# Attention scores: one float32 product per head in place of three float32r products

## The chip, the cores and the metric

One core of one Trainium2 chip runs the whole program. The metric is the device time of one execution in microseconds (us); the kernel is launched once per execution, and of several executions the median counts. Engines are called PE (matrix products; PEld is its loading of the stationary operand), DVE (vector), ACT (scalar), POOL and SP (which issues most of the DMAs).

## What is computed

Windowed attention with global keys and a linear bias, and then two feed-forward layers with different gates:

```python
scores = scale * np.matmul(q, k.transpose(0, 1, 3, 2))   # (2, 8, 768, 64) each
scores = scores + bias                                   # -slope(head) * distance
scores = np.where(keep, scores, -1000000000.0)           # 96 local keys, 8 global ones
a = softmax(scores);  attn = np.matmul(a, v)
x = attn as (1536, 512)
x = silu(x @ w_in) @ w_out                # weights (512, 2048), (2048, 512), float64
out = (h * clip(h + 3, 0, 6) / 6) @ w2_out,  h = x @ w2_in
```

## The kernel before

The program has two stages that overlap a little. The attention (some 0 to 143 us of the profile) is cut into 16 units: a batch entry, half of the sequence (384 queries) and a pair of heads. A unit has three tiles of 128 queries, so that there are 48 steps `n` (list `seq`). After it come the feed-forward layers, whose pieces are long chains of PE products with the weights split into a high and a low float32r half; from step 16 on, every second step of the attention also carries one such piece (`h_piece`, 12 products, or `y_piece`).

A step is spread over several turns of the loop (`attention_loop`, `transposes`), and one turn issues, in this order: `stage_b` of tile n (scores into PSUM tiles `psS`, one bank per head; DVE adds the bias and takes the minimum into `z`; ACT takes exponentials); `stage_b2` of tile n-1 (DVE makes the reciprocal sums `sm`, POOL scales `z`); the deferred work in `rests`; `stage_c` of tile n-3 (four PE transposes of `z` into `psT`, copied to `pt` by DVE, or by ACT in a unit's first tile); `stage_d` of tile n-4 (products of `pt` and the values into `psO`); a feed-forward piece; and, once a unit each, `stage_a` for the keys (part 0) and the queries (part 1) of a later unit.

`stage_a` (L321) transposes three 128x128 tiles of two heads' keys or queries on PE, with the keys before the block and the 32 global keys (`kp`) as one more small transpose, into a PSUM bank `psA`. Two heads lie one above the other, in partitions 0 to 63 and 64 to 127. ACT then writes the high half (`kh` at L366 in two or three pieces, `qh` at L337 with the scale -1/8), in float32r, and one turn later DVE writes the rest to `kl` (L370, as many pieces) and `ql` (L340). Pieces: 128x384 for the own keys, 128x64 for the two copies of the global keys between them, and in second halves 128x128 for the keys before the block. `stage_b` (L379) makes three products for each of the two heads, `qh kh`, `qh kl` and `ql kh`, all of 256 key columns, alternating between the heads (L385 to L388).

Orders: PE, ACT and POOL execute in the order in which the code issues (`manual_schedule`, L799). DVE and the DMA queue of SP are ordered by the framework's scheduler while the attention runs, and by the code after it. PSUM has eight banks: two of tag `S` for the scores, three of tag `tr` that `psA` and `psT` share, two `o`, one `f`. `raw` tiles of keys, queries and weights have two buffers, and a load waits until the old content has been read.

Of the kernel before, what the change touches and what calls it, by code (L numbers as in the profile page):

```python
# [10 lines left out]
F32 = mybir.dt.float32  # L11
F32R = mybir.dt.float32r
# [3 lines left out]
ALU = mybir.AluOpType  # L16
PSUM = bass.MemoryType.PSUM

P = 128
# [9 lines left out]
def attention_ffn_kernel(ctx, tc, q, k, v, n_global, n_local, w_in1, w_out1, w_in2, w_out2, out):  # L29
    nc = tc.nc  # L30
    B, H, S, D = q.shape
# [4 lines left out]
    HB = 3  # L36
    TB = HB * P
# [19 lines left out]
    apool = first_half.enter_context(tc.tile_pool(name="att", bufs=2, side="right"))  # L57
# [4 lines left out]
    def bank(tag, name):  # L62
        return psum.tile([P, 512], F32, name=name, tag=tag, bufs=ps_bufs[tag])
# [153 lines left out]
    raw, tr = {}, {}  # L217
    G = NGLOB_MAX
    ZB = 4
    G0 = P - G  # L220
    W = 2 * P
# [77 lines left out]
    def beyond():  # L299

        fl, ng, nl = small[:, 2:5], nval[:, 0:1], nval[:, 1:2]
        nc.vector.tensor_scalar(out=fl[:, 0:1], in0=nl, scalar1=1.0, scalar2=None, op0=ALU.is_lt)
        nc.vector.tensor_scalar(out=fl[:, 1:2], in0=nl, scalar1=float(NLOC_MAX), scalar2=None, op0=ALU.is_gt)
        nc.vector.tensor_scalar(out=fl[:, 2:3], in0=ng, scalar1=float(NGLOB_MAX), scalar2=None, op0=ALU.is_gt)
        nc.vector.tensor_tensor(out=fl[:, 0:1], in0=fl[:, 0:1], in1=fl[:, 1:2], op=ALU.add)
        nc.vector.tensor_tensor(out=fl[:, 0:1], in0=fl[:, 0:1], in1=fl[:, 2:3], op=ALU.add)
        nc.vector.tensor_copy(flag, fl[:, 0:1])
# [3 lines left out]
    def biases(p):  # L311

        nbs[p] = [cpool.tile([P, 2, w], F32, name=f"{n}{p}", tag=f"{n}{p}") for n, w in (("nbB", P), ("nbA", W))]
        for nb, dist in zip(nbs[p], (distB, distA)):
            for h in range(2):
                nc.gpsimd.tensor_scalar(out=nb[:, h, :], in0=dist, scalar1=slopes[2 * p + h], scalar2=1.0, op0=ALU.mult, op1=ALU.mult)


    KW = P + HB * SP

    def stage_a(u, part):  # L321

        b, half, p = units[u]
        rk, kp, rq, rv, vp = raw[u]
        if part == 0:
            tr[u] = tuple(apool.tile([P, w], F32R, name=f"{n}{u}", tag=n) for n, w in (("kh", KW), ("kl", KW), ("qh", TB), ("ql", TB)))
        kh, kl, qh, ql = tr[u]
        ps = bank(ATAG, f"psA{u}_{part}")
        src = rq if part else rk
        for i in range(HB):  # L330
            nc.tensor.transpose(ps[:, i * P:(i + 1) * P], src[:, i].rearrange("p h d -> p (h d)"), ident)
        sub = dict(op0=ALU.mult, op1=ALU.subtract)
        if part:
            sc = -1.0 / (D ** 0.5)

            def evac():
                nc.scalar.mul(qh, ps[:, :TB], sc)  # L337

            def rest():
                nc.vector.scalar_tensor_tensor(out=ql, in0=ps[:, :TB], scalar=sc, in1=qh.bitcast(F32), **sub)  # L340

            return evac, rest
        m = TB + (P if half else G)
        kpf = kp.rearrange("p h d -> p (h d)")
        if half:
            nc.tensor.transpose(ps[:, TB:m], kpf, ident)
        else:
            nc.tensor.transpose(ps[:, TB:m], kpf[:G], ident[:G, :G])

        def tiles(x):  # L350
            return x[:, P:].rearrange("p (t c) -> p t c", t=HB)

        def own(x):
            return x.rearrange("p (t c) -> p t c", t=HB)

        def glo(x):
            return x.unsqueeze(1).to_broadcast([P, HB - 1, G])


        parts = [(lambda x: tiles(x)[:, :, :P], own(ps[:, :TB])), (lambda x: tiles(x)[:, :HB - 1, P:], glo(ps[:, m - G:m]))]  # L360
        if half:
            parts.append((lambda x: x[:, :P], ps[:, TB:m]))

        def evac():
            for at_, src in parts:
                nc.scalar.copy(at_(kh), src)  # L366

        def rest():
            for at_, src in parts:
                nc.vector.tensor_tensor(out=at_(kl), in0=src, in1=at_(kh).bitcast(F32), op=ALU.subtract)  # L370

        return evac, rest

    zt, smt, ptt, pso = {}, {}, {}, {}

    def first(u, t):
        return units[u][1] == 0 and t == 0

    def stage_b(n, u, t):  # L379
        b, half, p = units[u]  # L380
        kh, kl, qh, ql = tr[u]
        tags = ("SS", "fS", "Sf")[n % 3] if n < PRE - 1 else "SS"
        ps = [bank(tags[h], f"psS{u}_{t}_{h}") for h in range(2)]
        o = P if first(u, t) else t * SP
        for i, (a, c) in enumerate(((qh, kh), (qh, kl), (ql, kh))):  # L385
            for h in range(2):
                hs = slice(h * D, (h + 1) * D)
                nc.tensor.matmul(ps[h][:, :W], a[hs, t * P:(t + 1) * P], c[hs, o:o + W], start=i == 0, stop=i == 2)  # L388
        w, nb = (P, nbs[p][0]) if first(u, t) else (W, nbs[p][1])
        z = apool.tile([P, 2, W], F32, name=f"z{u}_{t}", tag="z", bufs=ZB)  # L390
        mn = apool.tile([P, 2], F32, name=f"mn{u}_{t}", tag="mn", bufs=3)
        sm = apool.tile([P, 2], F32, name=f"sm{u}_{t}", tag="sm", bufs=3)
        for h in range(2):
            nc.vector.tensor_tensor_reduce(  # L394
                out=z[:, h, :w], in0=ps[h][:, :w], in1=nb[:, h, :], scale=1.0, scalar=3e38,
                op0=ALU.add, op1=ALU.min, accum_out=mn[:, h:h + 1])
        for h in range(2):
            nc.scalar.activation(out=z[:, h, :w], in_=z[:, h, :w], func=AF.Exp, bias=mn[:, h:h + 1], scale=-1.0,  # L398
                                 accum_out=sm[:, h:h + 1])
        zt[u, t], smt[u, t] = z, sm  # L400

    def stage_b2(u, t):
        z, sm, w = zt[u, t], smt.pop((u, t)), P if first(u, t) else W
        nc.vector.tensor_scalar(out=sm, in0=sm, scalar1=1e-9, scalar2=None, op0=ALU.add)  # L404
        nc.vector.reciprocal(sm, sm)  # L405
        for h in range(2):
            nc.gpsimd.tensor_scalar(out=z[:, h, :w], in0=z[:, h, :w], scalar1=sm[:, h:h + 1], scalar2=1.0,  # L407
                                    op0=ALU.mult, op1=ALU.mult)
# [34 lines left out]
    queue, late, rests, now = {}, {}, {}, [0]  # L443
# [4 lines left out]
    def attention_loop(n):  # L448
        for f in queue.pop(n, []):
            f()  # L450
        if n < len(seq):
            u, t = seq[n]
            stage_b(n, u, t)
            if t == HB - 1 and u + 1 < NP:
                biases(u + 1)
        if n == 0:
            e, r = stage_a(1, 0)
            e()
            r()
            beyond()  # L460
        if 0 <= n - 1 < len(seq):
            stage_b2(*seq[n - 1])
        for f in rests.pop(n, []):
            f()
        if APOS == 0:
            transposes(n)
        if 0 <= n - CL < len(seq):
            stage_c(*seq[n - CL])
        if 0 <= n - LAG < len(seq):
            u, t = seq[n - LAG]  # L470
            f = stage_d(u, t)
            if f:
                at(n + 1, f)
                if u + 2 < len(units):
                    loads_v(u + 2)

        if APOS == 1:
            transposes(n)

    def transposes(n):  # L480
        for d, part in ((KOFF, 0), (QOFF, 1)):
            if (n + d) % HB == 0 and 1 <= (n + d) // HB < len(units):
                e, r = stage_a((n + d) // HB, part)
                e()
                rests.setdefault(n + 1, []).append(r)
                if part and (n + d) // HB + 2 < len(units):
                    loads((n + d) // HB + 2)

# [237 lines left out]
    for l, c in chunks:  # L726
        first_piece[l, c] = len(stream)
        if fast(l, c):
# [5 lines left out]
            h, y = H(l, c, 2), Y(l, c, 0)  # L734
# [3 lines left out]
        if (l, c) == (1, 0):  # L738

            h = H(l, c, 0) + H(l, c, 1) + H(l, c, 2)  # L740
# [5 lines left out]
        for tk in blocks(l, c):  # L746
            hs = [(h_piece, l, c, tk, j) for j in range(FC)]
# [14 lines left out]
    with tc.manual_schedule(engines=None):  # L762
        nc.vector.memset(three, 3.0)
        for i, ap in enumerate((n_global, n_local)):
            nc.sync.dma_start(nwords[:, i, :], ap.bitcast(I32).partition_broadcast(P))
        loads(0)
        make_identity(nc, ident)
        positions()
        loads(1)
        load_weights()  # L770
        loads_v(0)
        load_weights()
        loads(2)
        loads_v(1)
        load_weights()
        ek, rk_ = stage_a(0, 0)
        ek()
        eq, rq_ = stage_a(0, 1)
        eq()
        patterns()  # L780
        rk_()
        rq_()
        biases(0)
    todo = {when(i): f for i, f in enumerate(stream)}

# [279 lines left out]
```

## Time and profile before

| what | us |
|---|---|
| executions timed | 641.52, 641.78, 646.76 (median 641.78) |
| span of the profiled execution, first to last instruction | 638.6 |
| busy in the span: PE / PEld | 617.2 / 498.9 |
| busy in the span: DVE / ACT / POOL | 489.9 / 417.4 / 161.0 |

The profiled execution's own device time isn't listed apart from its span; the two executions that agree end some 3 us above that span. Busy times are unions of an engine's instructions; the ends of PE's products are modelled and overlap, so that a busy PE need not be at its peak: how long a group of products occupies PE is read from where it starts to where the next one starts.

### The profile page before, as it was taken

The numbers are of one execution on the slowest core, as the hardware profiler recorded it, in microseconds if no ns is written. First come the engines' busy times: TensorE is split into PE (matmuls) and PEld (weight loads), VectorE is DVE, ScalarE is ACT, GpSimd is POOL, SyncE is SP. The second block draws the span as 40 slices with busy tenths as digits, with TensorE's granted clock in tenths as the row PEclk, the third lists the DMA queues.
The fourth block names the chain that finished last, engine by engine and source line by source line (L and its number), as shares of the span: only waits on it lengthen the run. The fifth ranks groups of instructions, "written<-read, shape, count | busy, mean of one in ns | idle before, by whom it ended". The sixth has DMA issues, their size and how long they took to land.

```text
span 638.6 us, 9729 instructions
## 1 busy us (share of the span) xinstructions
PE 617.2 (97%) x3214; PEld 498.9 (78%) x3214; DVE 489.9 (77%) x1107; ACT 417.4 (65%) x887; POOL 161.0 (25%) x233
## 2 busy tenths in 40 slices
PE   5889999999999999999999998999999999999996
PEld 3667777789888788888888887887788888888885
DVE  5899889953578796767675679988979696969453
ACT  4787877765557576666666676765766666666760
POOL 2776666561111111111212120011111111111110
PEclk9999999999999999999999999999999999999999
DMA  6555645349577667777776793186576868686544
GB/s 174 136 139 136 149 112 137 99 150 204 103 162 166 144 146 176 161 180 166 181 163 134 164 198 100 66 247 150 132 173 165 182 157 181 157 176 162 100 102 166
DMA packets 81625, 97.31 MB, mean 152 GB/s; under 512 B 55456, under 2 KB 55456, under 8 KB 81312
## 3 DMA queue, kind: packets, MB, share of 16 engines
q0 software_dynamic: 12576, 45.09, 37.7%
q1 hardware_dynamic: 68992, 51.53, 26.8%
q8 instruction: 27, 0.44, 0.3%
q14 instruction: 30, 0.25, 0.1%
HBM read 46.27 MB, written 3.15 MB: 77 GB/s over the span
## 4 chain that ended last, share of the span: by engine, by line
PE 35%; issue 25%; POOL 5%; DVE 2%; DMA 2%; ACT 1%; POOLq 0%; ACTq 0%; SPq 0%; DVEq 0%
PE psY L683 19%; PE psH L510 9%; POOL y L712 5%; PE psP_b L591 3%; PE psP_c L591 2%; PE psP_a L591 2%; DMA y<-st 1%; DMA raw<-in_moe_w_in_dram 1%; ACT st L708 0%; DVE g L541 0%; DVE da L1027 0%; DVE wol L148 0%; DVE dc L134 0%; DVE u L608 0%; ACT da L103 0%
## 5 line engine op out<-in xcount | busy, mean ns | idle before, releaser
L712 POOL DMA_DIRECT2D y<-st x78 | 66.9, 857 | 362.4 <-ACT st L708 357.2
L708 ACT COPY st<-psY 128x512 f32<-128x512 f32 x156 | 91.3, 586 | 51.6 <-PE psY L683 47.5
L510 PE MATMUL psH<-xh,wih 128*128 128x512 f32 (+1 forms) x216 | 83.2, 385 | 1.7 <-DVE g L541 1.7
L510 PE MATMUL psH<-xl,wih 128*128 128x512 f32 (+1 forms) x216 | 82.5, 382 | 0.0
L510 PE MATMUL psH<-xh,wil 128*128 128x512 f32 (+1 forms) x216 | 82.4, 382 | 0.0
L683 PE MATMUL psY<-gh,woh 128*128 128x512 f32 (+1 forms) x160 | 61.4, 384 | 0.0
L683 PE MATMUL psY<-gh,wol 128*128 128x512 f32 (+1 forms) x160 | 60.6, 378 | 0.0
L683 PE MATMUL psY<-gl,woh 128*128 128x512 f32 (+1 forms) x160 | 60.5, 378 | 0.0
L398 ACT ACTIVATE z<-z,mn 128x256 f32<-128x256 f32 (+1 forms) x96 | 46.5, 486 | 21.1 <-DVE mn L394 15.6
L407 POOL TENSOR_SCALAR z<-z,sm 128x256 f32<-128x256 f32 (+1 forms) x96 | 48.2, 514 | 43.9 <-DVE sm L405 18.4
L683 PE MATMUL psY<-woh,gl 128*128 128x512 f32 x144 | 56.1, 390 | 0.1
L683 PE MATMUL psY<-woh,gh 128*128 128x512 f32 x144 | 56.1, 390 | 0.1
L683 PE MATMUL psY<-wol,gh 128*128 128x512 f32 x144 | 56.0, 389 | 0.0
L510 PEld LDWEIGHTS psH<-xh,wih 128*128 128x128 f32 x216 | 40.5, 188 | 10.6 <-DVE g L541 2.1
L103 ACT ACTIVATE da<-raw 128x512 f32<-128x512 f32 x64 | 42.9, 670 | 5.9 <-DMA raw<-in_moe_w_in_dram 5.5
L510 PEld LDWEIGHTS psH<-xl,wih 128*128 128x128 f32 x216 | 40.5, 188 | 7.5 <-DVE xl L620 0.4
L510 PEld LDWEIGHTS psH<-xh,wil 128*128 128x128 f32 x216 | 40.5, 188 | 7.1
L1027 DVE SCALAR_TENSOR_TENSOR da<-raw,da 128x512 int32<-128x512 int32 x64 | 44.3, 693 | 1.2 <-DVE sm L404 0.2
L608 DVE TENSOR_TENSOR u<-psP_c,u 128x512 f32<-128x512 f32 x22 | 15.1, 688 | 34.5 <-ACT u L602 34.5
L532 ACT ACTIVATE a<-psH 128x512 f32<-128x512 f32 (+1 forms) x24 | 14.2, 590 | 40.4 <-PE psH L510 40.3
L551 DVE SCALAR_TENSOR_TENSOR gl<-a,gh 128x512 fp32r<-128x512 f32 (+1 forms) x34 | 23.2, 682 | 21.9 <-ACT gh L545 21.6
L1015 DVE TENSOR_SCALAR da<-da 128x512 f32<-128x512 f32 x64 | 28.3, 442 | 14.7 <-ACT da L103 14.7
(185 smaller groups left out, 1565.2 us busy)
## 6 DMA issues: line engine op xcount, KB each, us to landing
y<-st POOLq DMA_DIRECT2D x78, 512.0 KB, 4.8
raw<-in_moe_w_in_dram SPq DMA_DIRECT2D x32, 512.0 KB, 4.1
raw<-in_moe_w_out_dram SPq DMA_DIRECT2D x32, 512.0 KB, 3.3
rk<-in_k_dram SPq DMA_DIRECT2D x32, 96.0 KB, 2.5
rq<-in_q_dram SPq DMA_DIRECT2D x32, 96.0 KB, 2.9
rv<-in_v_dram SPq DMA_DIRECT2D x32, 96.0 KB, 2.6
out_dram<-y SPq DMA_DIRECT2D x12, 256.0 KB, 2.0
xf<-xh SPq DMA_DIRECT2D x2, 1024.0 KB, 6.7
```

The source lines that it names most:

```text
L103: nc.scalar.activation(out=t["a"], in_=raws[n][:, :, 1].bitcast(F32), func=AF.Abs)
L398: nc.scalar.activation(out=z[:, h, :w], in_=z[:, h, :w], func=AF.Exp, bias=mn[:, h:h + 1], scale=-1.0, accum_out=sm[:, h:h + 1])
L407: nc.gpsimd.tensor_scalar(out=z[:, h, :w], in0=z[:, h, :w], scalar1=sm[:, h:h + 1], scalar2=1.0, op0=ALU.mult, op1=ALU.mult)
L510: nc.tensor.matmul(ps, a[:, kt, js], x[:, kt, n0:n1], start=n == 0, stop=n == 3 * KT - 1)
L551: nc.vector.scalar_tensor_tensor(out=gl[:, j, :], in0=t["a"], scalar=2.0, in1=gh[:, j, :].bitcast(F32), op0=ALU.mult, op1=ALU.subtract)
L591: nc.tensor.matmul(ps, a[:, 2 * k + q, f * P:(f + 1) * P], x, start=p in (1, 5) and n == 0, stop=n == 5, skip_group_check=True)
L608: nc.vector.tensor_tensor(out=u, in0=st["c"], in1=u, op=ALU.add)
L683: nc.tensor.matmul(ps[:, :rhs.shape[1]], lhs, rhs, start=n == 0, stop=n == 3 * FC - 1)
L708: nc.scalar.copy(st[:, m % 2, :], part)
L712: late.setdefault(n, []).append(lambda: nc.gpsimd.dma_start(y, st, accum_op=ALU.add))
L1015: nc.vector.tensor_scalar(out=a, in0=a, scalar1=as_float(897 << 20), scalar2=as_float((1151 << 20) - 1), op0=ALU.max, op1=ALU.min)
L1027: nc.vector.scalar_tensor_tensor(out=ai, in0=w1, scalar=-0x40000000, in1=ai, op0=ALU.bitwise_and, op1=ALU.bitwise_or)
```

## The change

Keys and queries are kept as one float32 tile each (`kt`, `qt`) instead of a high and a low float32r tile. ACT writes the own keys and the queries as before, without the cast; the narrow pieces of the keys, the global ones and those before the block, are copied by DVE in the same turn instead of by ACT; DVE's subtractions are gone. The scores of a head are one float32 product of 256 columns.

```diff
@@ stage_a @@
-            tr[u] = tuple(apool.tile([P, w], F32R, name=f"{n}{u}", tag=n) for n, w in (("kh", KW), ("kl", KW), ("qh", TB), ("ql", TB)))
-        kh, kl, qh, ql = tr[u]
+            tr[u] = tuple(apool.tile([P, w], F32, name=f"{n}{u}", tag=n) for n, w in (("kt", KW), ("qt", TB)))
+        kt, qt = tr[u]
...
-            def evac():
-                nc.scalar.mul(qh, ps[:, :TB], sc)
-
-            def rest():
-                nc.vector.scalar_tensor_tensor(out=ql, in0=ps[:, :TB], scalar=sc, in1=qh.bitcast(F32), **sub)
-
-            return evac, rest
+            nc.scalar.mul(qt, ps[:, :TB], -1.0 / (D ** 0.5))
+            return
...
-        parts = [(lambda x: tiles(x)[:, :, :P], own(ps[:, :TB])), (lambda x: tiles(x)[:, :HB - 1, P:], glo(ps[:, m - G:m]))]
+        nc.scalar.copy(tiles(kt)[:, :, :P], own(ps[:, :TB]))
+        nc.vector.tensor_copy(tiles(kt)[:, :HB - 1, P:], glo(ps[:, m - G:m]))
         if half:
-            parts.append((lambda x: x[:, :P], ps[:, TB:m]))
-
-        def evac():
-            for at_, src in parts:
-                nc.scalar.copy(at_(kh), src)
-
-        def rest():
-            for at_, src in parts:
-                nc.vector.tensor_tensor(out=at_(kl), in0=src, in1=at_(kh).bitcast(F32), op=ALU.subtract)
-
-        return evac, rest
+            nc.vector.tensor_copy(kt[:, :P], ps[:, TB:m])
@@ stage_b @@
-        for i, (a, c) in enumerate(((qh, kh), (qh, kl), (ql, kh))):
-            for h in range(2):
-                hs = slice(h * D, (h + 1) * D)
-                nc.tensor.matmul(ps[h][:, :W], a[hs, t * P:(t + 1) * P], c[hs, o:o + W], start=i == 0, stop=i == 2)
+        for h in range(2):
+            hs = slice(h * D, (h + 1) * D)
+            nc.tensor.matmul(ps[h][:, :W], qt[hs, t * P:(t + 1) * P], kt[hs, o:o + W], start=True, stop=True)
@@ transposes @@
-                e, r = stage_a((n + d) // HB, part)
-                e()
-                rests.setdefault(n + 1, []).append(r)
+                stage_a((n + d) // HB, part)
```

The calls of `stage_a` in the first turn and ahead of the loop change in the same way: before, the deferred halves `rk_()` and `rq_()` came after `patterns()`; now there are none.

## Rows read from the trace of the kernel before

**Rows 1.** The page's head: span of the profiled execution.

```profile
span 638.6 us, 9729 instructions
```

**Rows 2.** Busy time by stage (count in brackets; last: granted clock, DMA share, GB/s).

```profile
core 0: us, PE busy (x) PEld busy (x) DVE busy (x) ACT busy (x) POOL busy (x), PEclk, DMA share, GB/s
0.00:143.00 143.00, 130.02 (x1061) 96.11 (x1062) 119.84 (x453) 102.59 (x330) 90.21 (x151) 1.00 0.54 136
143.00:300.00 157.00, 156.48 (x704) 130.94 (x704) 110.61 (x198) 97.88 (x181) 24.30 (x28) 1.00 0.72 160
```

**Rows 3.** Chain that ended last, one of its feed-forward pieces: start, length, what.

```profile
422.07 2.72 PE psH L510 x12
```

**Rows 4.** Waits of PE from 20 to 143 us: total, times, longest.

```profile
PE psO L435 <- DVE pt L419: 2.9, 3, 1.1
PE psA L331 <- DMA rk<-in_k_dram: 0.9, 1, 0.9
PE psT L416 <- DVE kl L370: 0.9, 2, 0.6
PE psT L416 <- ACT pt L421: 0.5, 1, 0.5
```

**Rows 5.** Groups by line and shape, 0 to 143 us: busy us, mean ns, idle before.

```profile
L419 DVE COPY pt<-psT 128x512 f32<-128x512 f32 x32 | 21.7, 678 | 0.8 <-PE psT L416 0.8
L388 PE MATMUL psS<-kh,qh 64*128 64x256 f32 x96 | 21.2, 401 | 1.1 <-ACT qh L337 0.6 <-DVE mn L394 0.4
L435 PE MATMUL psO<-pt,rv 128*64 128x128 f32 x192 | 19.3, 277 | 0.0
...
L370 DVE TENSOR_TENSOR kl<-psA,kh 128x384 fp32r<-128x384 f32 x16 | 8.8, 548 | 0.7 <-ACT kh L366 0.7
L340 DVE SCALAR_TENSOR_TENSOR ql<-psA,qh 128x384 fp32r<-128x384 f32 x16 | 8.7, 546 | 0.0
...
L370 DVE TENSOR_TENSOR kl<-psA,kh 128x64 fp32r<-128x64 f32 x16 | 3.4, 209 | 0.0
L366 ACT CAST kh<-psA 128x64 fp32r<-128x64 f32 x16 | 3.3, 209 | 0.0
```

**Rows 6.** Timeline of PE, parts of 60 to 68 us: start, length, what.

```profile
60.70 0.64 PE L388 MATMUL psS<-kh,qh 64*128 64x256 f32 x2
...
61.51 0.66 PE L416 MATMUL psT<-ident,z 128*128 128x128 f32 x4
...
67.27 0.39 PE L388 MATMUL psS<-kh,qh 64*128 64x256 f32 x2
67.50 0.28 PE L388 MATMUL psS<-kl,qh 64*128 64x256 f32 x2
67.62 0.28 PE L388 MATMUL psS<-kh,ql 64*128 64x256 f32 x2
67.82 0.44 PE L416 MATMUL psT<-ident,z 128*128 128x128 f32 x2
```

**Rows 7.** Timeline of PE, moments at 62.10 us (first row) and 62.48 us.

```profile
62.09 0.33 PE L435 MATMUL psO<-pt,vp 128*64 128x128 f32 x2
...
62.25 0.28 PE L435 MATMUL psO<-pt,vp 128*64 128x128 f32 x2
62.36 0.39 PE L435 MATMUL psO<-pt,rv 128*64 128x128 f32 x4
```

**Rows 8.** Timeline of PE around one wait (idle time and its end in brackets).

```profile
34.91 0.66 PE L416 MATMUL psT<-ident,z 128*128 128x128 f32 x4
36.56 0.51 PE L435 MATMUL psO<-pt,vp 128*64 128x128 f32 x4 [0.99 <-DVE pt L419]
```

**Rows 9.** Timeline of DVE in that wait.

```profile
35.31 0.55 DVE L340 SCALAR_TENSOR_TENSOR ql<-psA,qh 128x384 fp32r<-128x384 f32 x1
35.77 0.15 DVE L405 RECIPROCAL sm<-sm 128x2 f32<-128x2 f32 x1
35.84 0.67 DVE L419 COPY pt<-psT 128x512 f32<-128x512 f32 x1
```

**Rows 10.** Timeline of PE, 13 to 24 us: two transposes that wait for keys.

```profile
14.97 0.87 PE L331 MATMUL psA<-ident,rk 128*128 128x128 f32 x3 [0.55 <-DMA rk<-in_k_dram]
...
23.24 0.52 PE L331 MATMUL psA<-ident,rk 128*128 128x128 f32 x3 [0.87 <-DMA rk<-in_k_dram]
```

More of the change, by code (lines that the diff above doesn't have):

```diff
@@ L331, in stage_a @@
             nc.tensor.transpose(ps[:, i * P:(i + 1) * P], src[:, i].rearrange("p h d -> p (h d)"), ident)
-        sub = dict(op0=ALU.mult, op1=ALU.subtract)
         if part:
-            sc = -1.0 / (D ** 0.5)
-            def evac():
-                nc.scalar.mul(qh, ps[:, :TB], sc)
-            def rest():
-                nc.vector.scalar_tensor_tensor(out=ql, in0=ps[:, :TB], scalar=sc, in1=qh.bitcast(F32), **sub)
-            return evac, rest
+            nc.scalar.mul(qt, ps[:, :TB], -1.0 / (D ** 0.5))
+            return
         m = TB + (P if half else G)
@@ L380, in stage_b @@
         b, half, p = units[u]
-        kh, kl, qh, ql = tr[u]
+        kt, qt = tr[u]
         tags = ("SS", "fS", "Sf")[n % 3] if n < PRE - 1 else "SS"
@@ L456, in attention_loop @@
         if n == 0:
-            e, r = stage_a(1, 0)
-            e()
-            r()
+            stage_a(1, 0)
             beyond()
@@ L482, in transposes @@
             if (n + d) % HB == 0 and 1 <= (n + d) // HB < len(units):
-                e, r = stage_a((n + d) // HB, part)
-                e()
-                rests.setdefault(n + 1, []).append(r)
+                stage_a((n + d) // HB, part)
                 if part and (n + d) // HB + 2 < len(units):
@@ L775, in attention_ffn_kernel @@
         load_weights()
[L776 to L779, printed above, removed]
+        stage_a(0, 0)
+        stage_a(0, 1)
         patterns()
-        rk_()
-        rq_()
         biases(0)
```

## The prediction

> **What bounds the kernel now.** I read the page first, then the busy time by stage, and then, in the attention, who waited for whom and the timelines of PE and DVE. The span is 638.6 us [rows 1]. The feed-forward stage leaves PE no room: from 143 to 300 us it is busy 156.48 of 157 us [rows 2], and the chain that ended last runs there from one PE piece into the next, such as twelve products in 2.72 us [rows 3]. The change touches nothing of that stage, which is of fixed length to within a microsecond; what it is worth is how much earlier or later the attention hands over at 143 us.
>
> In the attention two engines are nearly full. DVE is busy 119.84 of 143 us, PE 130.02 [rows 2]. PE's busy time can't be trusted by itself, so I looked for its waits: after 20 us they are few, 2.9 us for DVE's copies of `pt`, 0.9 for keys from memory, 0.9 for a bank that `kl` still read, 0.5 for ACT's copy of `pt`, 5.2 us in all [rows 4]. Some more hides inside groups of score products: six products normally occupy PE from 67.27 to 67.82, 0.55 us, but from 60.70 to 61.51, 0.81 us, where the second head's bank came free late [rows 6]. I found five such groups between 39 and 74 us, some 1.2 us together. So PE loses about 6.4 us to others in 123 us, and apart from these its own order of work sets the pace: what frees DVE can give back 6.4 us at most, and whatever lengthens PE's groups is paid nearly in full.
>
> **The change part by part.**
>
> *The score products.* Removed are six records of 256 columns a tile: one per float32r product, 96 of each of the three kinds for 48 tiles and two heads [rows 5]. They run in pairs, one head in the upper and one in the lower 64 rows: two records start together at 67.27, two at 67.50, two at 67.62 [rows 6]. A pair's slot is 0.12 us, the first is 0.11 longer for its weights, and some 0.08 pass before the next group, which makes up the 0.55.
>
> Added are two float32 products a tile. The nearest rows are those of `psO`, float32 already: 192 records for 96 products with `rv` [rows 5], so two records a product. They run in pairs too, where the heads use different 64 columns: two at 62.09, two at 62.25, the next at 62.36 [rows 7]. A slot is 0.11 us for 128 columns, twice what float32r takes per column; for 256 columns I take 0.22. If the heads run side by side, the group is 0.11 for the weights, two slots of 0.22, and 0.08 at the end: 0.63 us, 0.08 more than now. Rounded up for the coarse reading: 0.09.
>
> The bounds. Below: a record as short as that of 128 columns, two slots of 0.11, group 0.41, which is 0.14 less than now. Above: heads one after the other, four slots of 0.22, group 1.07, 0.52 more. I take the side-by-side case, since float32r pairs of exactly this geometry (64 rows each) run so and float32 pairs with the other split run so; only the combination isn't shown. 48 tiles by 0.09 is 4.3 us. The first five tiles, before 20 us, run at about half the pace and so gain up to 0.2 us each, but PE there waits 0.55 and 0.87 us for keys from memory [rows 10], whose DMAs don't hang on the scores, and that hides them. If that cover went, they would cost 1 us. The other 43 cost 3.9 us.
>
> The rows on `psO` show one thing more: two records start together though a float32 product needs two records in turn. The Trainium skill, page "TensorE: Matmul & The Clock Gate", Part 3, section "The mechanism", says that matmuls keep the program's order in start and end, "strict FIFO, no reordering". By that rule, with a product's two records next to each other in the queue, the second record of the first head would hold back the other head. The pairs at 62.09 and 62.25 speak against this, or for records that are already interleaved in the queue; it stays as a rival below.
>
> *DVE's subtractions.* The 16 wide ones for `kl` and 16 for `ql` go, 8.8 and 8.7 us of DVE [rows 5]. The narrow subtractions of `kl` turn into copies of the same shape. A copy from PSUM isn't shown at 64 columns; the subtraction takes 209 ns, and 678 ns for a copy of 512 columns bounds it above [rows 5]. I take 209, a change of nothing; the upper end, 24 narrow copies at 0.47 more, would be 11 us of DVE against the 17.5 that go, so DVE gains either way.
>
> What this gives to PE: in the wait of [rows 8], PE is ready for `psO` at about 35.5 and gets `pt` at 36.56. DVE executes `ql` at 35.31, and the copy of `pt` follows at 35.84 [rows 9]: without `ql` it comes 0.46 us earlier. Three waits of this kind make the 2.9 us [rows 4]; `ql` alone gives 1.4, `kl` as well gives more where DVE hadn't caught up with PE in between. I take 1.9 (bounds 1.4 and 2.9). In what is left, the next late thing is DVE's `z` and `xl` ahead of `pt`. The 0.9 us behind `kl`: the bank `psA` is now free after a copy instead of a subtraction one turn later, but its last reader is still a DVE instruction in a long queue; I take 0.6. The slow score groups: DVE reads the old scores earlier; 0.7 of 1.2.
>
> *ACT.* It loses the narrow copies, 3.3 us for the 64-column ones [rows 5]. ACT isn't what PE waits for, apart from one 0.5 us [rows 4]; I take 0.3 of it.
>
> *The waits that are added.* A score product now waits for ACT's and DVE's copies into the same `kt`. If DVE's narrow copy is held until ACT's wide one has written that tile, DVE's queue stands, with `pt` and the minima behind it. In the old order the corresponding wait, `kl` for `kh`, cost 0.7 us in all [rows 5], and the keys are transposed at least three turns ahead of use; I take nothing, with 0.7 as the upper end. No DMA is issued in another place. The start of the kernel gains up to 0.6 us before the wait for keys at 14.97 and loses it there.
>
> *Sum.* Plus 3.9 for the products; minus 1.9, 0.6, 0.7 and 0.3, together 3.5. Net +0.4 us. The profiled execution has 638.6 us of span and some 3 around it, so 641.6, in line with the median of 641.78: forecast 642.0. With all bounds of this case except the products' slot, from all 6.4 us of waits and the 0.9 of the cover recovered (641.6 + 3.9 - 6.4 = 639.1, less some at the start) to only `ql`'s 1.4 recovered and the start's 1 us paid (645.1, with the 0.7 for ACT 645.8): 638 to 646.
>
> **The rivals.**
>
> *Staggered heads* (slower). Each product's two records stand together and are executed strictly in turn, so head two begins when head one's second record does: three slots instead of two, group 0.85, 0.30 more than now. 48 by 0.30 is 14.4 us; PE is then so far the slower engine that DVE's waits vanish, 5 us: 651. It decides as soon as a group takes over 0.70 us, where 43 groups cost more than the 6.4 there are to recover. For it: the plain expansion of a product into two records. Against: [rows 7].
>
> *Heads one after the other* (slower). With 64 rows, a float32 product keeps the other half from running. Group 1.07: 48 by 0.52 is 25 us, less 6: 660.6. For it: float32 with row halves isn't in the trace. Against: nothing in float32r's pairs at 67.27 needs the number format.
>
> *Cheap records* (faster). What takes 0.11 us in `psO` is a fixed price of a record, or its weights, and 256 columns take little more. Group 0.41: 43 by 0.14 is 6 us less, and the waits on DVE shrink as well, some 4 (PE is faster, so DVE binds earlier): 631.6. For it: only one width of float32 is seen. Against: float32r products lengthen with their columns.
>
> *All stalls gone.* Side-by-side heads, but DVE's 17.5 us take out every wait, and the loads of keys behind the weights' decoding come earlier too: 638. It is the low end of the forecast's own case.
>
> **How the numbers follow.** Forecast 0.65, all stalls gone 0.08, staggered 0.10, one after the other 0.10, cheap 0.07. About 1% (6.4 us) is what a measurement of this kernel can tell from no change. Faster by more: cheap, 0.07. Slower by more: the two slow rivals, 0.20. The rest, 0.73, is within 1%. The likeliest case's own range is 638 to 646; to leave out no more than 2 in 10 I go up to take in the staggered heads and leave out one-after-the-other and cheap, 0.17: 636 to 653.
>
> **What would show it.** In the changed profile, `psS` should have 192 records of 256 columns instead of 288, in pairs about 0.22 us apart, and the group should take some 0.63 us. A second head's record 0.2 us behind the first one's is the staggered rival, 0.4 us behind is the serial one. DVE should be busy 16 to 18 us less before the hand-over, PE's waits for `pt` should fall from 2.9 to about 1 us, and the first dense feed-forward piece should start within 4 us of 143. The prediction is wrong if the group is longer than 0.70 or shorter than 0.50, or if the hand-over moves by more than 4 us while the group is as said: then a wait that I priced at nothing decides.

## The result: 1% slower, and the two places where it went

The changed kernel took 648.62 us (median of 15 executions, 645.57 to 652.75) against 641.93 for the kernel before (15 executions, 640.45 to 646.88): ratio 1.0095, 95% interval 1.0076 to 1.0113. That is inside the predicted range, outside the likeliest case's own range (638 to 646), and 6.6 us above the forecast of 642.0.

The profiled executions lie further apart: the span is 648.1 us, against 638.6 [rows 1]. With the 1.8 us that lie around a span (649.87 device time and 648.1 span here), before's profile was an execution of about 640.4, 1.5 below its median, and after's is 1.25 above its own. So a single profile of this kernel places a moment to some 2 us (an estimate from these two), and sizes below are taken from ratios, or from differences inside one trace.

The page's span, and the busy time in the form of [rows 2], up to the last product of the attention (149.19 us) and in the feed-forward stage; below it the kernel before, up to its own last product of the attention:

```profile
span 648.1 us, 9476 instructions
```

```profile
0.00:149.19 149.19, 138.04 (x951) 92.08 (x952) 106.28 (x420) 99.10 (x303) 88.10 (x150) 0.99 0.53 131
```

```profile
143.00:300.00 157.00, 156.26 (x731) 130.61 (x730) 107.35 (x192) 98.62 (x184) 28.15 (x31) 1.00 0.71 156
```

```profile
0.00:140.46 140.46, 127.52 (x1047) 93.85 (x1048) 119.29 (x452) 100.13 (x327) 89.07 (x150) 1.00 0.53 131
```

DVE is busy 13.0 us less in the attention (106.28 against 119.29). The feed-forward stage is as full as it was. PE is busy longer: 138.04 against 127.52. Of DVE's waits from 20 to 143 us the first line is now one for PE, of which there was little before (total, times, longest; after, then before):

```profile
DVE z L376 <- PE psS L370: 16.2, 15, 4.2
```

```profile
DVE z L394 <- PE psS L388: 1.5, 5, 0.5
```

The timeline of PE in a quiet stretch, to be set beside [rows 6]:

```profile
36.77 0.70 PE L370 MATMUL psS<-kt,qt 64*128 64x256 f32 x4
37.41 0.66 PE L398 MATMUL psT<-ident,z 128*128 128x128 f32 x4
```

A score group runs from 36.77 to 37.41; by the records' own starts it is 0.632 us, where the six float32r products took 0.55. Four records of 256 columns in 0.63 leave no room for three slots (0.85) or four (1.07): the heads run side by side, their records starting some 7 ns apart, and a head's second record 0.32 us after its first. The rule of the Trainium skill that the prediction set beside this ("TensorE: Matmul & The Clock Gate", Part 3, "The mechanism": "strict FIFO, no reordering") doesn't make the second head wait for both records of the first: by the 7 ns the trace speaks against that reading of it. The four records of a group have no one fixed order. At step 14 the second head's bank comes late; the first head's two records (the second of them gives the product's closing signal) go ahead, and the other head's two follow when its bank is free:

```profile
44.42 0.70 PE L370 MATMUL psS<-kt,qt 64*128 64x256 f32 x2
45.30 0.70 PE L370 MATMUL psS<-kt,qt 64*128 64x256 f32 x2 [0.19 <-DVE mn L376]
45.93 0.33 PE L398 MATMUL psT<-ident,z 128*128 128x128 f32 x1
```

That group takes 1.51 us. The one at step 20 does the same and takes 1.44.

The groups by shape, 0 to 150 us (the form of [rows 5]), and PE's waits from 20 to 150 us (the form of [rows 4]):

```profile
L370 PE MATMUL psS<-kt,qt 64*128 64x256 f32 x192 | 40.1, 469 | 1.2 <-ACT qt L333 0.6 <-DVE mn L376 0.5
...
L353 DVE COPY kt<-psA 128x64 f32<-128x64 f32 x16 | 3.5, 217 | 4.8 <-ACT kt L352 4.8
```

```profile
PE psO L417 <- DMA vp<-in_v_dram: 2.1, 3, 1.2
PE psT L398 <- DVE kt L353: 1.0, 1, 1.0
PE psS L370 <- DVE mn L376: 0.5, 2, 0.3
PE psO L417 <- DVE pt L401: 0.2, 1, 0.2
```

192 score records instead of 288, narrow copies at 217 ns, and PE's 2.9 us of waits for `pt` are down to 0.2: all that is as said. But three waits stand there that weren't before: DVE idles 4.8 us ahead of its narrow copy, PE waits 2.1 us for values from memory, and 1.0 for the narrow copy.

The place in the attention where the time goes shows when the two traces are laid beside each other by step: how much later than before the score group of step n starts, and how much later the last `psO`, after which the dense feed-forward chain runs (us; before's own moments in the first line; the lines under after are experiments told below, one profile each).

| kernel | n=1 | 5 | 8 | 12 | 16 | 17 | 46 | last psO | 17 to 46 |
|---|---|---|---|---|---|---|---|---|---|
| before, at | 11.78 | 20.57 | 27.35 | 37.81 | 47.27 | 51.38 | 128.22 | 140.46 | |
| after | -0.67 | +2.08 | +4.97 | +2.95 | +3.10 | +7.07 | +8.13 | +8.73 | +1.06 |
| float32 products alone | -0.66 | +0.54 | -0.12 | +0.10 | +0.19 | +0.17 | +2.59 | +3.03 | +2.42 |
| no subtractions | -0.87 | +0.91 | -0.02 | -0.78 | +0.86 | +0.76 | -0.84 | -0.45 | -1.60 |
| narrow copies on ACT | -0.70 | +0.46 | -0.20 | -1.19 | +0.22 | +0.56 | +1.80 | +2.12 | +1.24 |
| patterns first | -0.22 | +0.72 | +0.06 | -1.16 | -1.01 | +1.65 | +2.69 | +3.27 | +1.04 |
| PE filled | -0.71 | +2.71 | +2.04 | +3.43 | +2.88 | +6.88 | +7.90 | +8.50 | +1.02 |
| one load fewer | -0.59 | +2.00 | +2.32 | +1.30 | +1.45 | +1.60 | +2.66 | +3.23 | +1.06 |
| both mends | -0.22 | +0.90 | +3.75 | +1.74 | +1.90 | +2.05 | +3.11 | +3.68 | +1.06 |
| ACT's copies, one load fewer | -0.69 | +0.83 | +1.75 | +1.04 | +1.20 | +1.19 | +2.41 | +2.99 | +1.22 |
| one float32r product | -1.32 | -0.13 | +1.96 | +0.98 | +0.76 | +1.25 | -5.72 | -5.78 | -6.97 |

The hand-over is 8.73 us later. Less 1.5 and 1.25, the distances of the two profiled executions from their medians, that is 6.0, in line with the 6.1 of the ratio. After's loss comes in two jumps: some 3 us by step 12, though the first group started earlier than before, and 4 us between steps 16 and 17. From 17 to 46 it grows by only 1.06.

**The first jump** begins with the start of DVE's queue. Timeline of DVE before, then after, then of POOL after (idle time and its end in brackets):

```profile
4.66 0.16 DVE L279 SCALAR_TENSOR_TENSOR small<-nwords 128x2 f32<-128x2 int32 x1 [2.29 <-DMA nwords<-in_n_local_dram]
```

```profile
7.19 0.23 DVE L353 COPY kt<-psA 128x64 f32<-128x64 f32 x1 [4.82 <-ACT kt L352]
7.33 0.15 DVE L279 SCALAR_TENSOR_TENSOR small<-nwords 128x2 f32<-128x2 int32 x1
...
9.81 0.17 DVE L295 COPY pat<-pat 128x32 f32<-128x32 f32 x1
```

```profile
9.99 0.60 POOL L316 TENSOR_SCALAR nbB<-distB 128x128 f32<-128x128 f32 x2 [8.11 <-DVE pat L295]
```

The first narrow copy stands ahead of `patterns()`, as in the code, and it waits for ACT's wide copy into the same tile. The chain at L279 makes the distances from which POOL makes the bias tiles `nbB` and `nbA`. It started at 4.66 before and starts at 7.33 now, and POOL starts on `nbB` 2.7 us later (9.99 instead of 7.33). Then PE and DVE, around 21 us:

```profile
18.75 1.23 PE L370 MATMUL psS<-kt,qt 64*128 64x256 f32 x4
21.01 1.08 PE L398 MATMUL psT<-ident,z 128*128 128x128 f32 x4 [1.04 <-DVE kt L353]
```

```profile
20.11 0.42 DVE L376 CUSTOM_DVE_ANT_0 z<-psS,nbA 128x256 f32<-128x256 f32 x1 [1.29 <-PE psS L370]
...
20.64 0.22 DVE L353 COPY kt<-psA 128x64 f32<-128x64 f32 x1
```

PE's next bank of tag `tr` is held by a 0.22 us copy that stands behind a `z`, which itself waited for PE's scores. And the records here are almost twice as long as at 36.77: a score group takes 1.155 us (the one from 16.33, for example) instead of 0.632. The spacing is double from the first products on, up to 30.8 us; before, up to 20.2. The granted clock column prints 1.00 there in both, but this isn't a reading: the trace's list of the granted clock begins with an entry at full clock, at 30.85 us (before: 20.18), and the view counts time without an entry as full. Spacing and first entry change together, so I take the double spacing for PE at the lower of its two levels, 1.2 of 2.4 GHz. PE's last stop ahead of the rise ended at 21.01 us here, and at 14.97 before [rows 10]. From 20 to 30 us PE is not idle, it is slow (after, then before):

```profile
20.00:30.00 10.00, 8.99 (x43) 5.34 (x44) 5.55 (x24) 4.44 (x16) 6.21 (x12) 1.00 0.37 74
```

```profile
20.00:30.00 10.00, 8.05 (x77) 5.48 (x77) 9.01 (x36) 6.70 (x23) 7.90 (x15) 1.00 0.69 172
```

43 records in 8.99 us, where before had 77 in 8.05 (a score group has six there and four here).

**The second jump.** Timeline of SP's queue, DVE, and PE:

```profile
44.56 0.48 SPq L252 DMA_DIRECT2D vp<-in_v_dram  x1
48.87 0.37 SPq L87 DMA_DIRECT2D raw<-in_moe_w_in_dram  x1
49.28 0.57 SPq L253 DMA_DIRECT2D vp<-in_v_dram  x1
```

```profile
48.14 0.67 DVE L1001 SCALAR_TENSOR_TENSOR da<-raw,da 128x512 int32<-128x512 int32 x1
```

```profile
52.99 0.40 PE L417 MATMUL psO<-pt,vp 128*64 128x128 f32 x2 [1.21 <-DMA vp<-in_v_dram]
54.06 0.29 PE L417 MATMUL psO<-pt,vp 128*64 128x128 f32 x1 [0.66 <-DMA vp<-in_v_dram]
...
54.61 0.59 PE L488 MATMUL psH<-xh,wih 128*128 128x384 f32 x1
...
58.18 0.34 PE L488 MATMUL psH<-xh,wil 128*128 128x384 f32 x1
58.45 0.70 PE L370 MATMUL psS<-kt,qt 64*128 64x256 f32 x4
```

A load of packed weights (`raw`, two buffers) waits until DVE's decoding at L1001 has read the old content, until 48.8, and half a load of values stands behind it for 4.2 us. In the kernel before, the scheduler had the two in the other order, and the second half followed the first at once:

```profile
44.36 0.46 SPq L253 DMA_DIRECT2D vp<-in_v_dram  x1
44.87 0.43 SPq L232 DMA_DIRECT2D rk<-in_k_dram  x1
46.20 0.38 SPq L87 DMA_DIRECT2D raw<-in_moe_w_in_dram  x1
```

PE stands still for 2.1 us, and the feed-forward piece after it runs slowly: 3.84 us from 54.61 to 58.45, where the other pieces of twelve products beside the attention take 2.28 to 2.31. Here the clock column shows it: 0.68 granted from 55 to 60 us, which is part of the time at 1.2 and part at 2.4 GHz. It fell after the two stops shown:

```profile
55.00:60.00 5.00, 5.00 (x26) 4.26 (x27) 0.82 (x4) 0.78 (x2) 2.17 (x3) 0.68 0.64 144
```

2.1 of waiting and 1.55 of slow products (3.84 less 2.29) make 3.65 of the jump's 3.97.

### The profile page after: what moved, and what is told of

Read it like the earlier page. It is cut to its first block, busy times and chain, and to the rows that moved or that the text cites. A ratio compares the mean times of both kernels' runs of the same rounds, so it can differ in the third digit from the quotient of the medians.

```text
span 648.1 us, 9476 instructions
## 1 busy us (share of the span) xinstructions
PE 627.7 (97%) x3118; PEld 497.1 (77%) x3118; DVE 476.8 (74%) x1075; ACT 416.3 (64%) x863; POOL 160.1 (25%) x233
## 4 chain that ended last, share of the span: by engine, by line
PE 35%; issue 24%; POOL 5%; DVE 2%; DMA 2%; ACT 1%; POOLq 0%; ACTq 0%; SPq 0%; DVEq 0%
PE psY L661 19%; PE psH L488 8%; POOL y L690 5%; PE psP_b L569 3%; PE psP_c L569 2%; PE psP_a L569 2%; DMA y<-st 1%; DMA raw<-in_moe_w_in_dram 1%; ACT st L686 0%; DVE g L519 0%; DVE da L1001 0%; DVE wol L148 0%; DVE u L586 0%; ACT da L103 0%; DVE dc L134 0%
## 5 line engine op out<-in xcount | busy, mean ns | idle before, releaser
L380 ACT ACTIVATE z<-z,mn 128x256 f32<-128x256 f32 (+1 forms) x96 | 46.5, 486 | 25.0 <-DVE mn L376 20.2
L389 POOL TENSOR_SCALAR z<-z,sm 128x256 f32<-128x256 f32 (+1 forms) x96 | 46.1, 494 | 50.5 <-DVE sm L387 15.8
L1001 DVE SCALAR_TENSOR_TENSOR da<-raw,da 128x512 int32<-128x512 int32 x64 | 44.0, 688 | 1.0
L376 DVE CUSTOM_DVE_ANT_0 z<-psS,nbA 128x256 f32<-128x256 f32 x80 | 32.1, 416 | 16.7 <-PE psS L370 15.6
L370 PE MATMUL psS<-kt,qt 64*128 64x256 f32 x192 | 40.1, 469 | 1.2 <-ACT qt L333 0.6
```

Of the source, the lines that this page charges most:

```text
L370: nc.tensor.matmul(ps[h][:, :W], qt[hs, t * P:(t + 1) * P], kt[hs, o:o + W], start=True, stop=True)
L376: nc.vector.tensor_tensor_reduce(out=z[:, h, :w], in0=ps[h][:, :w], in1=nb[:, h, :], scale=1.0, scalar=3e38, op0=ALU.add, op1=ALU.min, acc ...
L1001: nc.vector.scalar_tensor_tensor(out=ai, in0=w1, scalar=-0x40000000, in1=ai, op0=ALU.bitwise_and, op1=ALU.bitwise_or)
```

## The experiments

Each was timed in the same batch as the kernel before, whose median was between 641.9 and 643.3 us in these batches. So the ratio is what counts: less 1, times 641.9, it gives microseconds against before. By it the change itself costs 6.1.

**The products alone.** The kernel before with float32 tiles and one product a head; the low halves are still made, by DVE, and not used.

```diff
-            tr[u] = tuple(apool.tile([P, w], F32R, name=f"{n}{u}", tag=n) for n, w in (("kh", KW), ("kl", KW), ("qh", TB), ("ql", TB)))
+            tr[u] = tuple(apool.tile([P, w], F32, name=f"{n}{u}", tag=n) for n, w in (("kh", KW), ("kl", KW), ("qh", TB), ("ql", TB)))
...
-        for i, (a, c) in enumerate(((qh, kh), (qh, kl), (ql, kh))):
-            for h in range(2):
-                hs = slice(h * D, (h + 1) * D)
-                nc.tensor.matmul(ps[h][:, :W], a[hs, t * P:(t + 1) * P], c[hs, o:o + W], start=i == 0, stop=i == 2)
+        for h in range(2):
+            hs = slice(h * D, (h + 1) * D)
+            nc.tensor.matmul(ps[h][:, :W], qh[hs, t * P:(t + 1) * P], kh[hs, o:o + W], start=True, stop=True)
```

> Products alone: keys and queries in float32 tiles, one float32 product a head, but ACT still writes all key pieces and DVE still makes its 40 + 16 subtractions one turn later (their results are left unused). Theory 'products': the group of scores is 0.63 us here as after the change, 43 of them cost 3.4 us, nothing else moves: 645 (644 to 646.5). Rival 'upset': longer products by themselves upset the order of DVE and of the loads as in the changed kernel, then most of its 7 us is here: 647 or more. Rival 'free': DVE is so far behind that the longer groups hide in PE's waits: 642 to 643.

Measured: 643.69 us, ratio 1.0014 (0.9993 to 1.0034), so +0.9 us (-0.4 to +2.2). From step 17 to 46 it falls 2.42 us behind before, which is 29 steps at 0.083: there the longer groups are paid in full, as far as one profile each tells. Up to step 17 nothing is lost (+0.17). In whole that is nearer to the rival 'free' (0 to 1.1 us) than to the theory (2.1 to 4.6). PE still waits 2.7 us for `pt`. The hand-over is 3.03 later than in before's profile; of that, up to 1.5 is that profile's being a quick one.

**The subtractions alone.** The kernel before without DVE's subtractions; three products of the high halves.

```diff
-                nc.vector.scalar_tensor_tensor(out=ql, in0=ps[:, :TB], scalar=sc, in1=qh.bitcast(F32), **sub)
+                pass
-            for at_, src in parts:
-                nc.vector.tensor_tensor(out=at_(kl), in0=src, in1=at_(kh).bitcast(F32), op=ALU.subtract)
+            pass
-        for i, (a, c) in enumerate(((qh, kh), (qh, kl), (ql, kh))):
+        for i, (a, c) in enumerate(((qh, kh), (qh, kh), (qh, kh))):
```

> Subtractions alone left out: three float32r products a head as before, all three of the high halves (the low halves are left out of the computation), ACT writes all key pieces, DVE has nothing to do for keys and queries. Theory 'relief': PE's waits for pt and for the bank fall, 2 to 3.5 us faster than before: 638.5 to 640. Rival 'upset': taking work from DVE changes the scheduler's order of DVE and of the loads so that new waits come in: 642 or slower.

Measured: 642.34 us, ratio 0.9988 (0.9963 to 1.0012). DVE is busy 17.0 us less up to the last `psO` (102.27 against 119.29; here it has no narrow copies either), and its relief alone is worth 0.8 us (2.4 faster to 0.8 slower), not told from nothing and short of the 2 to 3.5 expected. PE's waits from 20 to 145 us say why:

```profile
PE psS L387 <- DVE mn L393: 2.2, 2, 1.2
PE psA L346 <- DMA kp<-in_k_dram: 0.9, 1, 0.9
PE psO L434 <- DVE pt L418: 0.4, 2, 0.3
```

The waits for `pt` go, from 2.9 to 0.4, and 2.2 for the minima, where there was nothing, take their place; for keys PE waits 0.9 here and 0.9 before. All of this lies up to step 17, where the kernel is 0.76 behind; from 17 to 46 it gains 1.60.

**The narrow copies on ACT.** After, with the two narrow copies given back to ACT:

```diff
-        nc.vector.tensor_copy(tiles(kt)[:, :HB - 1, P:], glo(ps[:, m - G:m]))
+        nc.scalar.copy(tiles(kt)[:, :HB - 1, P:], glo(ps[:, m - G:m]))
-            nc.vector.tensor_copy(kt[:, :P], ps[:, TB:m])
+            nc.scalar.copy(kt[:, :P], ps[:, TB:m])
```

> The changed kernel with its narrow key copies put back on ACT; nothing else. Theory 'narrow': the 5 us beyond the products' price come from DVE's narrow copies (they wait for ACT ahead of the patterns at the start, and hold banks in the middle), so this gives 641.5 to 644. Rival 'loads': they come from a weight load that stands ahead of the values in the DMA queue and waits for DVE, whatever engine copies: 647 to 649, with PE waiting for vp near 53 us again.

Measured: 643.38 us, ratio 1.0008 (0.9987 to 1.0028), as its theory says. Neither jump is there (0.22 behind at step 16, 0.34 from 16 to 17), and the loss of after is gone: the products and the subtractions together are level with before, within some 2 us. A weight load stands in the way in SP's queue here too, of keys this time (`raw` at 40.89, `kp` at 41.30), which costs PE one wait of 1.1 us.

**Patterns first.** After, with only the first narrow copy issued behind `patterns()`:

```diff
+        if u == 0:
+            return lambda: nc.vector.tensor_copy(tiles(kt)[:, :HB - 1, P:], glo(ps[:, m - G:m]))
         nc.vector.tensor_copy(tiles(kt)[:, :HB - 1, P:], glo(ps[:, m - G:m]))
...
-        stage_a(0, 0)
+        narrow = stage_a(0, 0)
...
+        narrow()
```

> The changed kernel with the very first narrow copy issued behind the patterns, as the subtractions were. Theory 'narrow' (start part): patterns finish 2.5 us earlier; if that is what sets the first steps, 645.5 to 647. Rival 'hidden': PE waits for keys from memory at 15 us in any case and nothing comes out: 648 to 649.

Measured: 645.03 us, ratio 1.0034 (1.0013 to 1.0054), a little better than its theory: moving one copy of 0.2 us is worth 0.6% (3.9 us, to within some 2 by the two intervals). At step 16 the kernel is 1.01 ahead of before, where after was 3.10 behind, and the first entry at full clock is at 20.9 us. The second jump is still there, 2.66, and so is its wait:

```profile
PE psO L419 <- DMA vp<-in_v_dram: 2.1, 2, 1.6
```

**Filling PE at the start.** The rival for the first jump was that only PE's slow records matter, and that more work for PE would end them sooner. After, with eight 128x128 transposes of the identity into a bank that nobody reads, at step 4:

```diff
+        if n == 4:
+            fill = bank("o", "fill")
+            for i in range(8):
+                nc.tensor.transpose(fill[:, :P], ident, ident)
```

> The changed kernel, with eight transposes of the identity put into PE's order behind the scores of step 4, into a bank that nobody reads: they add nothing to the computation and fill PE's wait for DVE's narrow copy at 20 us. Theory 'pace': what costs is less the wait of 1 us than that PE stays at half pace until 30 us after it; with the wait filled the full pace comes at 20 to 24 us and the hand-over 2 to 4 us earlier: 644.5 to 647. Rival 'wait': the wait itself and what follows from it cost, the pace stays low or doesn't matter: 648 to 650, the fill's 1.7 us at half pace paid on top where it doesn't fit.

Measured: 650.95 us, ratio 1.0121 (1.0088 to 1.0155), no better than after and on the side of the rival 'wait'. The first entry at full clock is at 23.1 us instead of 30.9, but the last `psO` is 8.50 behind before. PE's waits:

```profile
PE psO L417 <- DMA vp<-in_v_dram: 1.9, 2, 1.5
PE psS L370 <- DVE mn L376: 1.5, 2, 1.2
```

The gain is there at step 8 (+2.04 against +4.97). Then PE waits for DVE at a minimum (1.2 us, until 31.29), its clock falls again (0.83 granted from 30 to 35 us and from 35 to 40, groups of 1.155 once more), and by step 16 the kernel is where after was (+2.88, +3.10). So ending the slow records sooner doesn't mend the first jump: DVE is late as well, PE meets it and slows again. What the slow records cost by themselves this run doesn't show.

**One weight load fewer ahead.** After, with two weight loads ahead of the loop instead of three, so that the loads stand one piece later in SP's queue. The missing one is issued at the decoding of weight piece 7, the last beside the attention (`n` counts weight pieces in this place, not steps of the attention).

```diff
         load_weights()
         load_weights()
-        load_weights()
...
+                if n == 7:
+                    load_weights()
```

> The changed kernel with one weight load fewer ahead of use while the attention runs (two before the loop instead of three, the missing one made up at the end), so that a load in SP's queue finds its buffer free when it comes up. Theory 'loads': the wait for vp near 53 us and the half-paced feed-forward piece behind it go, 3 to 4 us: 644.5 to 646. Rival 'start': the loss is all from the start, the loads only show it: 647.5 to 649.

Measured: 644.59 us, ratio 1.0032 (1.0008 to 1.0055), as the theory 'loads' says. The second jump is gone, from 3.97 to 0.15. SP's queue and PE's waits:

```profile
44.88 0.46 SPq L255 DMA_DIRECT2D vp<-in_v_dram  x1
...
49.84 0.42 SPq L87 DMA_DIRECT2D raw<-in_moe_w_in_dram  x1
```

```profile
PE psT L400 <- DVE kt L355: 1.0, 1, 1.0
...
PE psO L419 <- DMA vp<-in_v_dram: 0.3, 1, 0.3
```

The values no longer stand behind the weights. The wait for the narrow copy and the late start (+2.00 at step 5) remain. But the first jump is smaller too in this profile (+1.45 at step 16, where after had +3.10), with the first entry at full clock at 24.8 us instead of 30.9, although the edit leaves the start of DVE's queue alone.

**Both mends.** Patterns first and one load fewer:

> Both mends together, first narrow copy behind the patterns and one weight load fewer ahead. If start and loads are what the change lost beyond its products, this is level with the kernel before or a little better: 640.5 to 643. If the narrow copies on DVE cost something in the steady part as well: 644 or more.

Measured: 641.71 us, ratio 0.9999 (0.9980 to 1.0019). By the ratios the one mend gives 3.9 us and the other 4.0, 7.9 in sum; together they give 6.2, all of the 6.1 that the change had cost. On top of the other each gives 2.1 or 2.2. Such a difference is good to some 2 us, so that it stays open how far the two overlap. Its profile (643.69 us, 2 above the median) still shows double spacing up to 29.6 us and 3.75 at step 8.

**ACT's copies and one load fewer:**

> Narrow copies on ACT, and one weight load fewer ahead. Theory 'loads': the 1.1 us wait for kp at 44 us goes, against the same without this mend: 641 to 642.5. Rival 'no cover': a load that is issued later arrives too late for the decoding of its piece, PE waits for weights instead: 643.5 or more.

Measured: 641.29 us, ratio 0.9988 (0.9969 to 1.0006). It is 0.2% below the version without the mend of the loads (1.0008); the intervals overlap. PE's wait of 1.1 us for `kp` is gone, as its theory says.

**The mend of the loads in the kernel before.** The same edit as above, in the kernel before.

> The kernel before with the one mend of the weight loads alone: two weight loads ahead of the loop instead of three, the third at step 7. It separates what the mend is worth by itself from what it repairs in the change. Theory 'repair' (the load stood in SP's queue ahead of a value load only because the change had shifted the scheduler's order): before has no such wait of PE for values, so the mend gives it nothing, 640 to 643.5, ratio 0.998 to 1.002, hand-over within 1 us of 140.5. Rival 'gain' (the mend relieves the queue for any kernel, and the change plus mend is level only because the mend pays for the longer score groups): 638 to 640, ratio 0.994 to 0.997, hand-over at 137 to 138.5, and then the change itself, like for like, still costs 3 to 5 us.

Measured: 642.97 us, ratio 1.0005 (0.9980 to 1.0030). The hand-over is 0.98 later than before's. The edit gives before nothing that can be told from noise, so it repairs what the change upset and isn't a gain that pays for the products.

**One float32r product.** ACT's copies and one load fewer, with float32r tiles for `kt` and `qt`:

```diff
-            tr[u] = tuple(apool.tile([P, w], F32, name=f"{n}{u}", tag=n) for n, w in (("kt", KW), ("qt", TB)))
+            tr[u] = tuple(apool.tile([P, w], F32R, name=f"{n}{u}", tag=n) for n, w in (("kt", KW), ("qt", TB)))
```

> The version with ACT's narrow copies and one weight load fewer ahead (641.3 us, group of scores 0.632 us, hand-over at 143.5), with keys and queries as float32r tiles and one float32r product per head: the low halves of keys and queries take no part in the scores. It tests whether PE's score group is paid in full, from below. Expected group from the float32r slots of before (0.11 for the weights, one slot of 0.12, 0.08 to the next): 0.31 to 0.35 us, 0.28 to 0.32 less than 0.632. Theory 'PE's order sets the pace': 43 groups by 0.30 come off the hand-over, 13 us less, at 130 to 132, and the time is 628 to 631, ratio 0.978 to 0.983. Rival 'DVE binds next': DVE's 104 us busy and POOL's and the memory's own pace take over once PE is faster; waits of PE for pt, mn and keys reappear with 5 us or more, the hand-over is at 135 to 139 and the time 633 to 638.

Measured: 635.95 us, ratio 0.9893 (0.9854 to 0.9932), last `psO` at 134.7. The timeline of PE has the short group:

```profile
63.77 0.39 PE L372 MATMUL psS<-kt,qt 64*128 64x256 f32 x2
64.08 0.66 PE L400 MATMUL psT<-ident,z 128*128 128x128 f32 x4
```

0.315 us, 0.317 less than with float32. It fits neither theory whole: the time is the rival's (633 to 638), the hand-over lies just between the two. From step 17 to 46 the kernel gains 8.2 us on its float32 twin, of the 9.2 that 29 groups at 0.317 make: there PE's order does set the pace. Up to step 17 it gains nothing, +1.25 against before, as +1.19 in the twin: there the records are at double spacing until 33.1 us, and PE's waits from 20 us on are 3.5 in all (ACT's and DVE's copies of `pt`, minima), not the 5 or more of the rival.

## Why the prediction was right or wrong

The time is inside the stated range, and the change is within 1%, as forecast. By the prediction's own sign it is wrong all the same: the group is as said, and the hand-over moved by 8.73 us in the profiles, about 6 between the medians, where more than 4 was to mean that a wait priced at nothing decides. That the range held is luck: its upper end had been raised to 653 for the staggered heads, which the trace excludes, and 648.62 lies outside the 638 to 646 of the case that came true.

- **The score products** came out as worked: 0.632 us a group for 0.63, side by side, 0.083 more than before. (The pairs stand 0.32 apart: the sign that named 0.22 had left out the 0.11 for the weights that the sum has.) In steps 17 to 46 it was paid in full (2.42 for 29 steps). "The other 43 cost 3.9 us" was too much before step 17: the products alone had lost 0.17 by then, and the whole kernel 0.9.
- **DVE's relief**: the narrow copies take 217 ns for 209, and the waits for `pt` fell from 2.9 to 0.2 where 1 was said. DVE is busy 13.0 us less before the hand-over and not 16 to 18: the 17.5 are a sum of records that overlap in part (in [rows 9] `ql` takes 0.55 and the next record starts 0.46 after it). For PE the relief was priced too high. Alone it gave 0.8 us and not 3.5: 1.60 from step 17 on, and before that the minima were late next. The 0.7 for the slow score groups didn't come at all: the groups of steps 14 and 20 alone take 1.51 and 1.44 us. Products and relief were too big by about the same, so that their difference, +0.4, came out by luck: the change with both mends is level with before, within 1.3 us.
- **"I take nothing, with 0.7 as the upper end"**, for the waits that are added, is the first step that failed. The wait of the narrow copy for ACT's wide one was named, but priced by the 0.7 us that `kl` waited for `kh` in the old order. It costs DVE 4.8 us, all at one place: the very first copy. Before, the deferred `rk_()` came behind `patterns()`; in the change the copy goes with `stage_a`, ahead of it, and there it executes. It is worth 3.9 us by the experiment that moves this one copy.
- **"The start of the kernel gains up to 0.6 us before the wait for keys at 14.97 and loses it there"**: the gain came (-0.67 at step 1). The cover was the load of keys at 14.97; the loss came from `patterns()`, `z` and the narrow copy at 21.01, which don't wait for that load. The prediction had the double spacing of the first 20 us down as a fact of the start; in after, where PE's last early stop came at 21.01 us and not at 14.97, it lasted to 30.8.
- **"No DMA is issued in another place"** is the second step that failed. It is true of the code and not of SP's queue, which the scheduler orders anew. One half load of values behind one load of weights: 4.0 us by the experiment that takes that load out of the way; in the traces the jump falls from 3.97 to 0.15.
- **All stalls gone** (638) wasn't met: where the mends take the long waits out, short ones for minima remain, the score groups with a late second bank, and double spacing for the first 25 to 30 us.
- **"Some 3 around it"**: a span and its own device time differ by 1.8 us here; before's profiled execution was one of 640.4. The base of 641.6 is 1.2 us high for that execution, and in line with the median by luck.
- **The staggered heads** and **one after the other**, the rivals on the slow side, are excluded by 0.632. The slower time had another cause, the one in the last sentence of the prediction, a wait that was priced at nothing.

What stays open: why the scheduler set the weight load ahead of the values in after and in the version with patterns first, and ahead of keys with ACT's copies. And the double spacing at the start ended between 20.0 and 33.1 us in the versions' profiles, one each. Versions that differ in the weight loads alone end it at 20.0 and 25.0 (ACT's copies), at 20.9 and 29.6 (patterns first), at 30.9 and 24.8 (after). How much it varies from execution to execution wasn't measured, so neither is its share of the first jump.

## What to carry to other kernels

When a change moves or removes instructions of an engine or a queue, write down the new order at the start and in the DMA queue, the code's or the scheduler's, before pricing anything: the first copy that stands in front of the chain which all others need, and the load that waits for a buffer in front of one that is needed sooner, each cost some ten times its own length or more (3.9 us for a copy of 0.23, 4.0 for an issue of 0.37). Price a relief of an engine by what PE waits for next, in each half of a stage by itself: the same 17 us of DVE's work gave nothing up to step 17, where the minima were late next, and 1.6 us behind it, where PE set the pace. And lay two traces beside each other by step; the jumps name the place.

## What was not expected of the hardware

- PE's records took double time from its first product up to 30.8 us in after, and up to between 20.0 and 33.1 us in the other versions, while the column of the granted clock printed 1.00: it counts the time ahead of the trace's first clock entry as full. From 55 to 60 us the same lengthening is in the column (0.68). The length of the records says it in both places.
- Two float32 products in different row halves start 7 ns apart and run record beside record where both banks are free (0.632 us), but the first one's two records don't wait for the second product where its bank is late (44.42 and 45.30 us).
- A stop of PE costs more than itself: 2.1 us of waiting for values were followed by a piece of 3.84 instead of 2.29 us.
